# A one-core attention and long-convolution kernel: rotated sines, a check at the end in place of a branch at the start, and a new order of the work

## The chip, the cores and the metric

The kernel runs on one core of one Trainium2 chip. The core has five instruction streams that this text names as the profile does: PE (TensorE: matmuls; its weight loads are the rows PEld), DVE (VectorE), ACT (ScalarE), POOL (GpSimd) and SP (SyncE, which only issues transfers here). Work passes between them through SBUF and through PSUM, whose eight banks the kernel uses as four slots of two banks. The metric is device time in microseconds (us) of one execution; lower is better. Times quoted from the profile are of one execution of the kernel before the change.

## What is computed

Attention over 4 batches, 8 heads, 768 positions and head width 64, and then a gated long convolution on the 512 columns that the heads make together:

```python
scores = scale * q @ k.T                       # per batch and head
mask = causal                                  # heads with is_retrieval
     or causal & (key < 4 | q - key < 64)      # the other heads
a = softmax(where(mask, scores, -1e9))
x = concat_heads(a @ v)                        # (4, 768, 512)
x1, x2, x3 = split(x @ w_proj)                 # three of (4, 768, 512)
conv = irfft(rfft(x2, axis=1) * rfft(filter_fft, axis=0)[None])
out = (x1 * conv * x3) @ w_out                 # (4, 768, 512), float32
```

## The kernel before, in words

After some constants (`opening`, L895) the kernel compares the flags `is_retrieval` with the pattern that it was written for (`check`, L1849) and leaves the result, one number, in `other`. L1862 loads that number into a register on all five engines, and L1863 branches: `general` serves any pattern, `patterned` (from L1036) the expected one. The data at hand has the expected pattern, so `patterned` is what runs and what the profile shows.

`patterned` treats the heads in 16 pairs n, four to a batch. For a pair, SP loads q, k and v (L1401, L1404, L1423; three buffers each), an engine casts q and k to bfloat16 (`cq`, `ck`, helper lines L1101 on DVE, L1103 on POOL, L1107 on ACT), and they are transposed: for the first eight pairs by PE (`T`, L1447), with a copy out of PSUM behind it (`E`), for the later eight by a DMA_TRANSPOSE that SP issues (L1457). `kx` and `vx` pick out the keys and values that the far blocks need. `sc` (L1492) makes blocks of scores, for pairs 0 to 3 with the mask added as a matmul of a table of large negative numbers, `btab` (`sb`, L1505; the table is made on POOL at L1165 to L1183 and scaled on DVE at L1187); `ex` (L1511) is the exponential on ACT, `mk` the other masks on DVE, `at` (L1556) the product with v, which carries a column of ones that yields the row sums, `rec` (L1562) their reciprocals, `nm` (L1573) the scaling.

The convolution over 768 positions is a real Fourier transform done with matmuls: attention's result is folded into symmetric and antisymmetric parts (`fd`, `fe`, `fA`, `fS`, `fb`, `fr`, helper line L1110 and L1601), multiplied by a table of cosines and sines `G` of 3 blocks of 128 positions (`W`, L1617), projected (`X`, L1660), multiplied by the filter's spectrum (`pa`, `pb`, `pc`), brought back with the transposed table `Gi` (`c`, L1725), gated with x1 and x3 (L1695; `g`, `cv`, `y`), and multiplied by `w_out` (`o`, L1758). The filter's own transform is `lfilt` (a load of 768 KB by POOL's queue, L1264), `fold` (L1281, L1285) and `F` (L1293). The table is made at the start: `turns`, `angle`, `wrap`, `size` and four groups of Sin on ACT (L1192 to L1214), each over all three blocks; `Gt` (L1254) transposes it on PE.

The order is written out by hand: `FAST` is a list of words such as `sc0.4@1` or `ck0/v`, operation, then PSUM slot (@0 to @3) or engine (/v DVE, /p POOL, /s ACT, /d transfer). Each engine runs its instructions in the order in which the list puts them, and waits at each for what it reads or overwrites. `BLANKS` (L120) gives the sizes of the filler groups: matmuls of 512 columns whose result nobody reads (L1143). The last 128 rows of the output (`HALVED`) are made in two halves of 256 columns (L1754), which are copied out of PSUM by DVE and ACT and stored by SP (L1776) and by ACT's own queue. L1897 is what ends the program on every engine.

## Time and profile before

| what | us |
|---|---|
| three runs | 188.15, 187.84, 187.33 |
| median | 187.84 |
| the profiled execution, its span | 188.0 |
| busy: PE, DVE, ACT, POOL | 171.7, 152.6, 143.3, 64.1 |
| HBM read, written (MB) | 24.64, 6.29 |

The span runs from the first to the last event of the profiled execution. An engine's busy time leaves out branches, register loads and the issuing of transfers. In the rows of instructions the columns are start, duration, engine, line, operation and tiles, and in square brackets the idle time before and what ended it; in the rows of waits they are the time waited in all, the number of times, and the longest. The chain of waits lists, in order of time, what the end of the program hung on.

### The profile page before, as it was taken

To read this page: it belongs to the slowest core of one execution; us is meant where nothing else is said; L and a number is where in the kernel's file an instruction comes from. 1 tells how busy PE (TensorE), PEld (TensorE's weight loads), DVE (VectorE), ACT (ScalarE), POOL (GpSimd) and SP (SyncE) were. 2 spreads that over 40 slices of the span, in tenths; PEclk is the share of its full clock that TensorE was granted. 3 is DMA by queue.
4 is the path that set the end of the run, shared out by engine and by line. 5 is a ranking of instruction groups with operands and counts; after the bars stand their busy time and mean duration, and the time that the engine had idled before them with its cause. 6 is when DMAs were issued, how large, how long until landed. Compare 5 with 4: busy or idle time off the path is not lost.

```text
span 188.0 us, 4376 instructions
## 1 busy us (share of the span) xinstructions
PE 171.7 (91%) x1688; PEld 103.9 (55%) x1704; DVE 152.6 (81%) x301; ACT 143.3 (76%) x191; POOL 64.1 (34%) x96
## 2 busy tenths in 40 slices
PE   0889996989999999999999999999999999999960
PEld 0346773644585556565556656475567644565430
DVE  6559676968999998998799999999799996388720
ACT  6689995879997998987999999899895526613330
POOL 3368750992080094443210111311406405400200
PEclk9999999999999999999999999999999999999998
DMA  5999999699999899999899988688942205300363
GB/s 182 309 271 281 194 187 287 151 260 228 218 210 203 180 192 210 184 232 234 193 249 257 225 180 176 137 138 225 127 125 55 112 2 157 122 3 0 113 248 104
DMA packets 77695, 33.67 MB, mean 179 GB/s; under 512 B 66850, under 2 KB 74082, under 8 KB 77666
## 3 DMA queue, kind: packets, MB, share of 16 engines
q1 hardware_dynamic: 74576, 30.29, 70.4%
q0 software_dynamic: 2944, 2.88, 10.1%
q8 instruction: 15, 0.25, 0.6%
q10 hardware_dynamic: 146, 0.13, 0.2%
q14 instruction: 14, 0.11, 0.2%
HBM read 24.64 MB, written 6.29 MB: 165 GB/s over the span
## 4 chain that ended last, share of the span: by engine, by line
PE 65%; DVE 14%; DMA 7%; POOL 4%; ACT 3%; issue 2%; SPq 0%; POOLq 0%; DVEq 0%
PE f_x_ps L1695 18%; PE f_X_ps L1660 10%; PE f_out_ps L1758 8%; PE f_c_ps L1725 7%; PE f_sc L1492 6%; PE f_att L1556 6%; DMA qk_ahead<-in_q_dram 4%; DMA f_qk_f<-in_q_dram 3%; DVE f_attn L1573 2%; ACT f_pT L1511 2%; PE f_W_ps L1617 2%; DVE f_P L1110 2%; PE f_sc L1505 2%; DVE f_fo L1110 1%; DVE turns L1736 1%
## 5 line engine op out<-in xcount | busy, mean ns | idle before, releaser
L1511 ACT ACTIVATE f_pT<-f_sc 128x1024 bf16<-128x1024 f32 (+3 forms) x68 | 58.7, 918 | 3.7 <-PE f_sc L1492 3.2
L1695 PE MATMUL f_x_ps<-f_xT,f_wproj 128*128 128x384 bf16 x256 | 46.7, 326 | 0.4 <-DVE f_attn L1573 0.3
L1695 PEld LDWEIGHTS <-f_wproj 128*128 128x128 bf16 x256 | 23.9, 98 | 16.5 <-issue 1.6
L1660 PE MATMUL f_X_ps<-f_wproj,f_xh 128*128 128x512 bf16 x92 | 22.3, 379 | 0.2
L1758 PE MATMUL f_out_ps<-f_wout,f_gy 128*128 128x512 bf16 x86 | 21.7, 379 | 0.3
L1492 PE MATMUL f_sc<-f_qkT 64*128 64x128 bf16 (+3 forms) x248 | 20.3, 250 | 0.0
L1725 PE MATMUL f_c_ps<-f_Gi,f_P 128*128 128x384 bf16 x96 | 18.4, 326 | 0.2 <-DVE f_gy L1714 0.2
L1110 POOL TENSOR_TENSOR f_fo<-f_attn 128x384 bf16<-128x384 bf16 x13 | 12.3, 954 | 15.0 <-DVE f_attn L1573 14.8
L1736 DVE TENSOR_TENSOR turns<-angle,f_c_ps 128x384 bf16<-128x384 f32 x32 | 16.3, 548 | 1.3 <-PE f_c_ps L1725 0.8
L1556 PE MATMUL f_att<-f_v_aug,f_pT 128*128 128x65 bf16 x392 | 17.2, 193 | 0.0
L1556 PEld LDWEIGHTS <-f_pT 128*128 128x128 bf16 x472 | 16.0, 97 | 2.1 <-issue 0.4
L1107 ACT COPY f_o<-f_out_ps 128x1024 f32<-128x1024 f32 (+2 forms) x12 | 10.2, 854 | 8.7 <-PE f_out_ps L1758 7.8
L1573 DVE TENSOR_TENSOR f_attn<-f_att,f_rec 128x768 bf16<-128x768 f32 x16 | 15.3, 955 | 0.6
L1492 PEld LDWEIGHTS <-f_qkT 64*128 64x128 bf16 x248 | 10.6, 94 | 9.3 <-issue 7.0
L1660 PEld LDWEIGHTS <-f_xh 128*128 128x128 bf16 x96 | 9.0, 98 | 10.3 <-issue 0.7
L1107 ACT CAST f_xh<-f_W_ps 128x768 bf16<-128x768 f32 x13 | 10.5, 807 | 4.5 <-PE f_W_ps L1617 2.3
L1758 PEld LDWEIGHTS <-f_gy 128*128 128x128 bf16 x92 | 8.6, 98 | 9.3 <-DVE f_gy L1718 0.3
L1107 ACT CAST f_X<-f_X_ps 128x1024 bf16<-128x1024 f32 x10 | 10.2, 1016 | 4.6 <-PE f_X_ps L1660 4.5
L1531 DVE TENSOR_TENSOR f_pT<-f_pT,mtab 128x1024 bf16<-128x1024 bf16 (+1 forms) x18 | 12.1, 688 | 1.4 <-ACT f_pT L1511 1.4
L1447 PE MATMUL f_qkT_ps<-identity,f_qk_bf 128*128 128x128 bf16 x96 | 7.9, 225 | 5.6 <-DVE f_qk_bf L1101 5.2
L1725 PEld LDWEIGHTS <-f_P 128*128 128x128 bf16 x96 | 9.0, 98 | 6.5 <-issue 0.6
L1110 POOL TENSOR_TENSOR f_br<-f_fo,f_uv 128x256 bf16<-128x256 bf16 x6 | 4.6, 765 | 21.3 <-DVE f_uv L1110 12.3
(132 smaller groups left out, 329.9 us busy)
## 6 DMA issues: line engine op xcount, KB each, us to landing
f_v_f<-in_v_dram SPq DMA_DIRECT2D x32, 192.0 KB, 4.4
out_dram<-f_o SPq DMA_DIRECT2D x17, 256.0 KB, 2.3
qk_ahead<-in_k_dram SPq DMA_DIRECT2D x6, 384.0 KB, 6.3
qk_ahead<-in_q_dram SPq DMA_DIRECT2D x6, 384.0 KB, 6.3
qk_ahead<-in_k_dram SPq DMA_DIRECT2D x10, 192.0 KB, 4.3
qk_ahead<-in_q_dram SPq DMA_DIRECT2D x10, 192.0 KB, 4.9
f_wproj<-in_moe_w_proj_dram POOLq DMA_DIRECT2D x6, 256.0 KB, 7.2
out_dram<-f_o SPq DMA_DIRECT2D x3, 512.0 KB, 4.4
```

The source lines that it names most:

```text
L1107: nc.scalar.copy(out=out, in_=in_)
L1110: (nc.gpsimd if now["engine"] == "p" else nc.vector).tensor_tensor(out, a, b, op)
L1492: nc.tensor.matmul(sc[:, bank, col:col + 128 * cnt], lhsT=keys, rhs=qkT(n)[rows, 0, 128 * i:128 * (i + cnt)], start=(col == 0 or not biase ...
L1511: nc.scalar.activation(out=pT(n)[:, c, :, 0:w], in_=held[f"sc.{n}.{c}"][:, :, 0:w], func=AF.Exp, scale=SCALE)
L1531: nc.vector.tensor_mul(some, some, near(c)[:, None].to_broadcast([128, 2, cols, 128]))
L1556: nc.tensor.matmul(att[:, hh, 65 * i:65 * i + 65], lhsT=pT(n)[:, c, bank, col:col + 128], rhs=values, start=(z == 0), stop=(z == len(here) ...
L1573: nc.vector.tensor_mul(attn(n).rearrange("p i hh d -> p hh i d"), rows[:, :, :, 0:64], held[f"rec.{n}"][:, :, :, None].to_broadcast([128, ...
L1660: nc.tensor.matmul(ps[:, u, :], lhsT=xh(b)[:, cc, chain, 128 * part:128 * part + 128], rhs=wproj()[:, cc, DM:2 * DM], start=(cc == 0), sto ...
L1695: nc.tensor.matmul(ps[:, s, 0:HS], lhsT=wproj()[:, cc, part * DM + cb * 128:part * DM + (cb + 1) * 128], rhs=xT(b)[:, cc, s * HS:s * HS + HS],
L1725: nc.tensor.matmul(ps[:, r, 0:HS], lhsT=P(b)[:, t, u, ch], rhs=Gi()[:, tile_no], start=(m == 0), stop=(m == 2))
L1736: fn(conv[:, half * HS:half * HS + HS], held[f"evs.{b}.{cb}"], held[f"c_ps.{b}.{cb}"][:, 1, 0:HS])
L1758: nc.tensor.matmul(ps[:, i % 2, :], lhsT=gy(b)[:, cb, i * 128:(i + 1) * 128], rhs=wout()[:, cb, :], start=(cb == 0), stop=(cb == NC - 1))
```

## The change

1. **One path in line.** `general` is rewritten as a slow version with loops whose transfers all go by GpSimd's queue. The branch at the start is gone; `patterned` always runs. At its end the kernel decides whether the result may stand: all reciprocals of row sums are kept in one array (`recs`), `gd0` to `gd2` on DVE test that each lies between 2^-100 and 2^100, `gd3` (a matmul of one column) counts the rows where that holds, `gd4` joins it with the flags' comparison, and `flag` loads it into a register on all engines; only if it is not 0 does `general` run behind. The mask table goes from 2^15 to 2^100 for this.
2. **Rotated sines.** Only the first of the three blocks of the table is made with `turns`, `wrap`, `size` and Sin; the other two follow by rotation by a third of a turn (`gc`, `gr`, `gm`, `gs`: a copy, scaled copies and scaled sums, most of them on DVE).
3. **Fillers.** Seven filler matmuls (`warm`) stand at the very start of PE's stream; the 17 that were in three groups are in eight.
4. **The last rows.** The two halves of the last 128 rows have a PSUM tile each.
5. **The order.** `FAST` is drawn up anew: engines, slots and order of many operations differ. The number of matmuls is the same but for the seven fillers and `gd3` (1704 before, 1712 now).

```diff
-BLANKS = (8, 3, 6)
+WARM = 7
+BLANKS = (2, 2, 2, 2, 3, 2, 2, 2)
+FAR = 2.0 ** 100
+LEAST = 2.0 ** -100
...
+    @op("warm")
+    def _():
+        ps = psum.tile([128, 512], FP32, name="warm")
+        for _ in range(WARM):
+            nc.tensor.matmul(ps, lhsT=blank()[:, 0:128], rhs=blank(), start=True, stop=True)
...
-            src = (size if part == 0 else angle)()[:, :, lo:hi].rearrange("p m (r f) -> p m r f", r=2)
+            src = (size() if part == 0 else angle()[:, 0])[:, lo:hi].rearrange("p (r f) -> p r f", r=2)
...
+    @op("gc")
+    def _():
+        ev(G()[:, :, 0], base())
+    for i in range(2):
+        scaled(f"gr{i}", lambda i=i: turned()[:, :, i], lambda i=i: base()[:, 1 - i:5 - i:3], KAPPA if i == 0 else -KAPPA)
+    for u in range(2):
+        for m in range(1, NM):
+            @op(f"gm{u}.{m}")
+            def _(u=u, m=m):
+                tiles = slice(3 * u, 3 * u + 2)
+                nc.vector.scalar_tensor_tensor(
+                    out=G()[:, tiles, m], in0=base()[:, tiles], scalar=0.5 if (u, m) == (0, 1) else -0.5,
+                    in1=turned()[:, u], op0=ALU.mult, op1=ALU.subtract if (u, m) == (1, 2) else ALU.add)
...
+    @op("gd0")
+    def _():
+        nc.vector.tensor_scalar(out=sane(), in0=recs().rearrange("p n h t -> p (n h t)"), scalar1=LEAST, scalar2=None,
+                                op0=ALU.is_ge)
...
+    @op("gd2")
+    def _():
+        nc.vector.tensor_reduce(out=right()[:, 0:1], in_=sane(), op=ALU.min, axis=mybir.AxisListType.X)
+    @op("gd3")
+    def _():
+        nc.tensor.matmul(banks("rows_right")[0:1, 0, 0:1], lhsT=right()[:, 0:1], rhs=v_aug(0)[:, 0, 0, 64:65],
+                         start=True, stop=True)
+    @op("gd4")
+    def _():
+        nc.vector.tensor_scalar(out=pre["other"], in0=held["rows_right"][0:1, 0, 0:1], scalar1=128.0,
+                                scalar2=pre["differ"], op0=ALU.not_equal, op1=ALU.max)
+    @op("flag")
+    def _():
+        pre["reg"] = nc.values_load(pre["other"][0:1, 0:1], min_val=0, max_val=1)
...
+                        ps = banks(f"out_ps.{b}.{i}.{half}")
...
+    patterned(tc, ahead, pre, q, k, v, int(n_sink), int(window), moe_w_proj, moe_filter_fft, moe_w_out, out)
+    with tc.If(pre["reg"] != 0, preferred_fallthrough_block=False):
+        general(tc, local, q, k, v, int(n_sink), int(window), moe_w_proj, moe_filter_fft, moe_w_out, out)
```

How the order changed is shown at four places. A row is line, operation, output tile, input tiles and shape of one instruction, or of several alike (x2).

On ACT, the stretch from the constants to the first exponential (`f_pT` is an exponential's output, `f_qk_bf` a cast q and k, `f_qkT` a transposed one, `f_G` and `f_base` the sines). Before:

```order
L1862 TENSOR_LOAD other
L1863 COMPARE_AND_BRANCH
L1192 ACTIVATE turns<-fcol,tfrac 128x384 x2
L1214 ACTIVATE f_G<-angle 128x3x2x64
L1107 COPY f_qkT_3005<-f_qkT_ps_2983 128x768
L1214 ACTIVATE f_G<-angle 128x3x2x128
L1214 ACTIVATE f_G<-f_size,quarter 128x3x2x64
L1107 CAST f_qk_bf_2972<-qk_ahead_68 128x768
L1214 ACTIVATE f_G<-f_size,quarter 128x3x2x128
L1107 COPY f_qkT_3051<-f_qkT_ps_3029 128x768 x2
L1511 ACT_TABLE_LOAD
L1511 ACTIVATE f_pT_3076<-f_sc_3_3048 128x2x384
```

and now:

```order
L552 CAST f_qk_bf_139<-qk_ahead_66 128x768
L471 ACTIVATE turns<-fcol,tfrac 128x384
L691 ACTIVATE f_base<-angle 128x2x64
L691 ACTIVATE f_base<-angle 128x2x128
L691 ACTIVATE f_base<-f_size,quarter 128x2x128
L552 COPY f_qkT_166<-f_qkT_ps_152 128x768
L684 ACTIVATE f_turned<-f_base 128x2x128
L691 ACTIVATE f_base<-f_size,quarter 128x2x64
L1006 ACT_TABLE_LOAD
L1006 ACTIVATE f_pT_199<-f_sc_4_188 128x1024
```

Four copies and casts stood among the sines, two stand there now, one of them the cast of the first k, and a scaled copy for the rotation; the sines are over one block and no longer three.

On POOL, from the first cast on (`mtab` is the mask table, `f_v_aug` the values with their column of ones, `f_kx` the picked keys; the last operand of a cast is the buffer of the load that it waits for). Before:

```order
L1103 CAST f_qk_bf_2972<-qk_ahead_68 128x768
L1103 CAST f_qk_bf_2974<-qk_ahead_65 128x768
L1383 MEMSET f_v_aug_2979 128x12
L1103 CAST f_qk_bf_3009<-f_qk_f_2_2977 128x768
L1379 MEMSET f_kx_3011 128x4x64
L1383 MEMSET f_v_aug_3036 128x12
L1165 AFFINE_SELECT mtab<-mtab 128x3x128
L1170 MEMSET mtab 4x128
L1171 AFFINE_SELECT mtab<-mtab 128x3x128
L1178 AFFINE_SELECT mtab<-mtab 128x3x128
L1183 MEMSET mtab 4x3x128
```

and now:

```order
L448 AFFINE_SELECT mtab<-mtab 128x3x128
L633 MEMSET mtab 4x3x128
L453 MEMSET mtab 4x128
L548 CAST f_qk_bf_139<-qk_ahead_66 128x768
L454 AFFINE_SELECT mtab<-mtab 128x3x128
L878 MEMSET f_v_aug_174 128x12
L704 TENSOR_SCALAR f_base<-par 128x1
L878 MEMSET f_v_aug_197 128x12
L878 MEMSET f_v_aug_206 128x12
L548 CAST f_qk_bf_208<-qk_ahead_69 128x768
L548 CAST f_qk_bf_249<-f_qk_f_2_135 128x768 x2
```

The mask table stood behind three casts, the last of them of pair 2 (`f_qk_f_2`); now only its last step stands behind one, of pair 0.

On SP, the loads and the first transposes by transfer of pairs 8 and up (`f_xT` and `f_Xw` are other tiles; the three `f_qkT` are of pairs 8, 9 and 10). Before:

```order
L1457 DMA_TRANSPOSE f_qkT_3844<-f_qk_bf_3842 128x12x128
L1404 DMA qk_ahead_65<-in_k_dram 128x6x64 x2
L1404 DMA qk_ahead_65<-in_q_dram 128x6x64 x2
L1423 DMA f_v_f_7_3972<-in_v_dram 128x6x64 x2
L1404 DMA qk_ahead_68<-in_q_dram 128x6x64 x2
L1423 DMA f_v_f_8_4076<-in_v_dram 128x6x64 x2
L1457 DMA_TRANSPOSE f_qkT_4099<-f_qk_bf_4094 128x12x128
L1423 DMA f_v_f_10_4274<-in_v_dram 128x6x64 x2
L1457 DMA_TRANSPOSE f_qkT_4282<-f_qk_bf_4161 128x12x128
```

and now:

```order
L899 DMA qk_ahead_66<-in_k_dram 128x6x64 x2
L918 DMA f_v_f_7_1183<-in_v_dram 128x6x64 x2
L952 DMA_TRANSPOSE f_qkT_1242<-f_qk_bf_1204 128x12x128
L899 DMA qk_ahead_69<-in_k_dram 128x6x64 x2
L952 DMA_TRANSPOSE f_qkT_1345<-f_qk_bf_1299 128x12x128
L918 DMA f_v_f_8_1355<-in_v_dram 128x6x64 x2
L899 DMA f_qk_f_11_1364<-in_k_dram 128x6x64 x2
L952 DMA_TRANSPOSE f_qkT_1458<-f_qk_bf_1382 128x12x128
```

The three transposes by transfer stood with ten loads between the first and the second; now two loads stand there, and they come closer together, behind more of the loads of pairs 8 to 10.

On DVE, the end of the program now (`f_c_ps` and `f_x_ps` are results of L1725 and L1695, `f_out_ps_5_0` and `f_out_ps_5_1` the PSUM tiles of the halves, `f_o` what is stored):

```order
L555 TENSOR_TENSOR turns<-turns,f_x1s_3_2886 128x768
L1213 TENSOR_TENSOR f_gy_2769<-turns,f_x_ps_3_2890 128x768
L661 TENSOR_SCALAR other<-f_rows_right,differ 1x1
L546 COPY f_o_0_2922<-f_out_ps_1_2900 128x512
L546 COPY f_o_2_2934<-f_out_ps_5_0_2916 128x256
L666 TENSOR_LOAD other
L546 COPY f_o_2_2934<-f_out_ps_5_1_2949 128x256
L1363 COMPARE_AND_BRANCH
```

Of these, the row of L661, the register load and the copy of one half by itself ahead of the other are new; the branch stands here and no longer at the start.

1036 lines of the change are left out of this document (288 added, 748 removed).

## The prediction

> **What bounds the kernel now.** I read the page first: the busy shares, the slices, the chain that ended last.
>
> ```profile
> PE 171.7 (91%) x1688; PEld 103.9 (55%) x1704; DVE 152.6 (81%) x301; ACT 143.3 (76%) x191; POOL 64.1 (34%) x96
> ...
> PE 65%; DVE 14%; DMA 7%; POOL 4%; ACT 3%; issue 2%; SPq 0%; POOLq 0%; DVEq 0%
> ```
>
> PE is busy for 91% and makes up 65% of the chain: what can be won is where it idles or runs fillers, or behind its last matmul, since the change keeps every matmul. The stretches show where (length, then busy time of PE, PEld, DVE, ACT, POOL, then PE's clock, the share of the DMA engines, GB/s).
>
> ```profile
> 0.00:8.00 8.00, 2.78 (x12) 1.46 (x13) 5.67 (x22) 4.58 (x8) 1.98 (x12) 1.00 0.70 221
> ...
> 16.00:24.00 8.00, 7.68 (x141) 5.64 (x141) 5.99 (x12) 7.75 (x11) 6.61 (x10) 1.00 1.02 244
> 24.00:32.00 8.00, 6.47 (x98) 4.52 (x100) 5.28 (x12) 6.78 (x9) 1.94 (x5) 1.00 0.98 234
> 32.00:40.00 8.00, 7.22 (x88) 4.37 (x89) 6.28 (x9) 5.14 (x7) 7.09 (x11) 1.00 0.89 191
> ...
> 80.00:112.00 32.00, 31.62 (x354) 19.60 (x353) 29.29 (x62) 29.38 (x38) 6.86 (x11) 1.00 1.05 224
> ```
>
> Between 80 and 112 us PE misses 0.38 of 32, but ACT and DVE are at 29.4 and 29.3 there and the transfers take the whole of the 16 DMA engines (1.05): a stage with PE first and three others close behind. PE's waits of the first 48 us, asked by themselves, and its first rows:
>
> ```profile
> PE f_qkT_ps L1447 <- DVE f_qk_bf L1101: 5.2, 1, 5.2
> PE f_F_ps L1293 <- DVE f_fold L1285: 1.4, 1, 1.4
> PE f_sc L1492 <- POOL f_kx L1103: 0.6, 1, 0.6
> PE f_sc L1505 <- DVE f_btab L1187: 0.5, 1, 0.5
> PE f_qkT_ps L1447 <- POOL f_qk_bf L1103: 0.4, 1, 0.4
> ```
>
> ```profile
> 5.22 0.80 PE L1447 MATMUL f_qkT_ps<-identity,f_qk_bf 128*128 128x128 bf16 x6 [5.22 <-DVE f_qk_bf L1101]
> 5.81 3.60 PE L1143 MATMUL f_blank_ps<-blank 128*128 128x512 bf16 x8
> ...
> 11.73 1.46 PE L1143 MATMUL f_blank_ps<-blank 128*128 128x512 bf16 x6
> ```
>
> After the 5.2 us for the first load these waits are only 2.9 us. But PE is busy with fillers too: 3.60 us for eight (0.45 each), 1.46 for six (0.24 each), while the kernel waits for the first scores.
>
> **The head.** The chain of waits shows why the first scores come late, and ACT's rows what that does.
>
> ```profile
> 3.78 5.97 DMA f_qk_f<-in_q_dram
> 9.80 0.82 POOL f_qk_bf L1103
> ...
> 13.20 0.41 DVE f_btab L1187
> 13.65 0.27 PE f_sc L1505 x2
> ```
>
> ```profile
> 8.89 0.82 ACT L1107 CAST f_qk_bf<-qk_ahead 128x768 bf16<-128x768 f32 x1
> ...
> 10.45 0.78 ACT L1107 COPY f_qkT<-f_qkT_ps 128x768 bf16<-128x768 bf16 x1
> ...
> 12.75 1.28 ACT L1511 ACT_TABLE_LOAD   x1
> 14.04 2.64 ACT L1511 ACTIVATE f_pT<-f_sc 128x768 bf16<-128x768 f32 x3
> ```
>
> ```profile
> L1214 ACT ACTIVATE f_G<-angle x2: 523/684/845, 6.5 to 7.6; 128x384 bf16<-128x384 f32 x1, 128x768 bf16<-128x768 f32 x1
> ```
>
> The mask table is queued on POOL behind the cast of pair 2, whose load lands at 9.75; so the first masked scores are at 13.65 and the first exponential at 14.04. Afterwards ACT is full (7.75 of 8 between 16 and 24 us). In the new order the table stands behind one cast of pair 0 only, and ACT has three sines of 384 columns or fewer where it had four over three blocks. Step by step: PE's first transposes at 5.2 show that k of pair 0 is in and cast by then; ACT's cast of 0.82 may end near 5.0, `turns` on ACT and `wrap` on DVE (384 columns each, at the 0.52 of a sine of that size 0.55 or so) at about 6.1. Three sines (0.31 for 128 columns, 0.42 for 256, on the line through the row's 0.52 and 0.85, so 1.15), a copy of 0.78, a scaled copy and the last sine (0.7 together) end near 8.7. The table load of 1.28 puts the first exponential at about 10.0, 4.0 us earlier. Its scores are ready: second cast on POOL (0.82) by 6, transposes and copy 0.6 + 0.95, scores about 8.1. Bounds: 2 us earlier if the scores wait for the sines' copy on ACT, 4.5 if all is at its shortest.
>
> ACT carries about 0.6 us of other work between these exponentials that it did not carry before (the order has `ks2` there and a cast of pair 3 near the end), so by the end of pairs 0 to 2's exponentials I count 3.4 us. PE does not win all of that: 18 transposes of the table (`Gt`) lay in its shadow and now come later, 1.0 us by the two chain rows that follow, and 0.3 is left for slots. **PE gains 2.1 us here** (1.0 to 3.2).
>
> ```profile
> 15.12 0.67 PE f_Gi_ps L1254 x12
> ...
> 22.92 0.34 PE f_Gi_ps L1254 x6
> ...
> 26.53 7.03 DMA qk_ahead<-in_q_dram
> 33.61 0.83 POOL f_qk_bf L1103
> ...
> 41.75 0.65 PE f_blank_ps L1143 x3
> ```
>
> **The next stage, 24 to 48 us.** PE waits 1.4 us for the filter's fold and 0.6 for a `kx`, which by the chain hangs on a load issued at 26.5 and a late cast at 33.6. The filter's load and those of pair 5 stand earlier in the new list; but DMA's share is 0.98 and 0.89 there, so earlier issue is shared out. I take both waits as gone (2.0), with nothing as the low end. The third group of fillers (0.65) goes too; six of the new fillers stand later, between real work, at 0.22 each: 1.3 us lost. Into PE's stream comes one matmul of one column, nothing. New waits in a plan that has not been seen: between nothing and 3 us; I take 0.75, the nearest rows being the waits above of 0.4 to 1.4, each alone.
>
> **The rotation, the guard and POOL.** The sums of the rotation, four of them, two scaled copies and four plain ones, are about 4 us on DVE at the price of its copies of 768 columns (0.55 to 0.96); DVE is idle for 1.7 to 2.7 of each 8 us quoted before 40, so they cost nothing unless the transform's first matmuls come before them. The guard on DVE is two passes of 192 columns and a reduction, under 1 us by the price of its smaller rows (a fold of 384 columns is 0.395, below), on an engine that is busy for 81% of the span and idles 0.99 us before its last copy (in the tail's rows). Cover gone, each is at most its own length. POOL takes 7 or so more of the gating and folding operations.
>
> ```profile
> L1110 POOL TENSOR_TENSOR f_fo<-f_attn 128x384 bf16<-128x384 bf16 x13 | 12.3, 954 | 15.0 <-DVE f_attn L1573 14.8
> L1110 DVE TENSOR_TENSOR f_fo<-f_attn 128x384 bf16<-128x384 bf16 x19 | 7.3, 395 | 0.2
> ```
>
> A fold is 0.56 us longer there, on an engine that is 34% busy: a longer chain to each transform, inside the 0.75 above.
>
> **PE's end** by the sum: 2.1 + 2.0 + 0.65 - 1.3 - 0.75 = 2.7 us earlier, 1.2 to 4.2 by the bounds taken together.
>
> **The tail.**
>
> ```profile
> 181.64 0.42 DVE L1101 COPY f_o<-f_out_ps 128x256 f32<-128x256 f32 x1 [0.99 <-PE f_out_ps L1754]
> 182.10 0.37 ACT L1107 COPY f_o<-f_out_ps 128x256 f32<-128x256 f32 x1 [0.70 <-DVE f_o L1101]
> 182.50 0.40 ACTq L1776 DMA_DIRECT2D out_dram<-f_o  x1
> ```
>
> ```profile
> L1863 ACTq COMPARE_BRANCH  x2: 38/42/45, 3.7 to 182.9; - x2
> ```
>
> ```profile
> L1897 ACTq DRAIN  x2: 8/44/80, 187.0 to 187.4; - x2
> out_dram<-f_o ACTq DMA_DIRECT2D x1, 128.0 KB, 3.0
> ```
>
> The last two copies share a PSUM tile and run one after the other; the tiles of their own let the first go out early, and only one copy of 0.42 and one store of 3 us stay behind the last matmul: 0.4 us gained (0.46 for the second copy, less the register loads, which took 0.47 to 0.54 at the start and now stand between copies). ACT leaves its last branch at 182.9 and does nothing until 187.0, 4.1 us, longer than the store needs (182.5 + 3.0 = 185.5): the end hangs on that idle stretch, behind a jump over the other block's code (some 180 rows on ACT). Now the jump is over about 40 rows. If the stretch stays at 4.1, ACT's earlier end is worth 0.4 to 0.8; if it goes, the store's landing decides, up to 1.8. I take **1.0**. [...] The branch at the start cost its row loads (about 0.5) off PE's path, since PE waits for the load of k there until 5.2.
>
> **Sum.** Profiled span 188.0 - 2.7 - 1.0 = 184.3; that execution lies 0.16 above the median of 187.84, so 184.1.
>
> **Rivals.**
>
> *A. Given back.* The head's 4 us only let PE run into the stage of 48 to 112 us earlier, where ACT, DVE and the transfers are at 0.91 to 1.05. For it: the three rows of load in that stretch; against: the new list takes copies and casts of some 5 us from ACT, PE was the one that others waited for. If the whole 2.7 is lost, the tail remains: 188.0 - 1.0 - 0.16 = 186.8; if half, 185.5; with new waits also eating the tail, 187.8.
>
> *B. Slower.* The transposes by transfer of pairs 8, 9 and 10.
>
> ```profile
> L1457 SPq DMA_TRANSPOSE f_qkT<-f_qk_bf x8: 1391/1665/3304, 56.0 to 123.0; - x8
> DMA to landing us min/median/max: 3.7/4.2/7.1
> ```
>
> ```profile
> 69.77 1.14 PE L1617 MATMUL f_W_ps<-f_G,f_fo 128*128 128x384 bf16 x6
> ```
>
> Now the first is issued at 56.0 and its scores come after these transform matmuls, at about 72: 16 us. In the new order some 4 us of PE's work lie between the two places (the projections, products and transforms in between at this trace's prices), and the first three stand almost back to back behind loads. At the median of 4.2 that just fits; at 7.1 each is 3.1 late, on PE's path, three times 9.3: 193. It decides from 1.6 us a transpose, where the gain is gone and 0.5% more (188.8). With two of three late: 184.1 + 6.2 = 190.3. [...]
>
> *C. Both ends at their best.* Waits of the early stage gone, no new ones, and the idle stretch at the end gone: 188.0 - 4.2 - 1.8 - 0.16 = 181.8.
>
> *D. The sines' part does nothing.* If the first scores wait for PE's transposes or copies, not for ACT, the head gains 2 rather than 4: PE 1.0 rather than 2.1, so 185.2; within the forecast's spread.
>
> **How the numbers follow.** Forecast with D's smaller head (183 to 186): 0.55. C (below 183): 0.13. A beyond half (186 to 188.8): 0.21, some 0.09 of it below 186.9. B: 0.11. About 0.5% is what a measurement of this kernel can tell from no change, 186.9 to 188.8. Faster: 0.55 + 0.13 + 0.09 = 0.77; within: 0.12; slower: 0.11. The range reaches from C's best, 181.8, into A, 187.6, and leaves out B and the rest of A.
>
> **What would show it.** The first exponential at 10 us, not 14, and the last of pair 2 three us earlier; no wait of over 0.5 us for the fold or `kx` before 45; the transforms' first matmuls not behind the rotated table; PE's busy share over 97% between 40 us and its end, with no wait on f_qkT of a later pair; the last matmul near 179; ACT's stretch behind L1363 shorter than 4.1. I am wrong if PE's end is later than 181, or if DVE or ACT is over 95% in 48 to 112 while PE falls below.

## The result, and the profile after

| | before | after |
|---|---|---|
| runs, us | 188.15, 187.84, 187.33, 187.65 | 193.65, 193.01, 193.45, 193.05 |
| median | 187.75 | 193.25 |
| ratio, 95% interval | | 1.0279 [1.0227, 1.0331] |
| span of the profiled execution | 188.0 | 191.5 |
| last matmul ends | 181.6 | 185.6 |

The change made the kernel slower by 5.5 us; 184.1 was forecast, and the range ended at 187.6. Run again beside the kernel before it gave 1.031 (below, `e9_after_again`). The two profiles lie only 3.5 us apart. In the runs of the kernel before that stand beside the experiments the time is 1.7 to 1.8 us above the span, and by that the profiled execution of before, with a span of 188.0, was some 2 us longer than a median one; the forecast took its span for a time near the median. Differences in place and length are read from the profiles here, the size of the loss from the medians. (The profile of `e3_fill` below is of an execution that the comparisons leave out as disturbed; only places are read from it.)

The page after, busy time, the clock by slices and the chain's shares:

```profile
PE 176.4 (92%) x1712; PEld 105.1 (55%) x1712; DVE 165.9 (87%) x318; ACT 140.6 (73%) x182; POOL 74.1 (39%) x98
...
PEclk9969999999999999999999999999999999999996
...
PE 75%; DVE 11%; DMA 5%; ACT 4%; issue 2%; DVEq 0%
```

PE is busier by 4.7 us with the same useful matmuls (the fillers take some 2.5 us more, a stretch of 3.41 us at half clock up to 1.7, and 16 matmul records of the profile before are missing, x1688 of 1704), DVE by 13.3 and POOL by 10. The clock has a dent in the third slice (0.50 is granted from 10.44 to 13.85 us). PE's waits over the whole program (time waited, times, longest):

```profile
PE f_blank_ps L593 <- DVE f_Gi L546: 1.9, 1, 1.9
PE warm L463 <- DVE blank L382: 1.5, 1, 1.5
PE f_sc L987 <- DVE f_xh L546: 1.4, 1, 1.4
PE f_qkT_ps L942 <- ACT f_qkT L552: 1.1, 1, 1.1
PE f_sc L987 <- DVE f_xT L546: 0.7, 1, 0.7
PE f_sc L987 <- DVE f_qkT L546: 0.7, 1, 0.7
PE f_qkT_ps L942 <- DVE f_qk_bf L546: 0.6, 1, 0.6
```

The waits for the fold and for `kx` are gone, as forecast. In their place PE waits for DVE four times behind the head (4.6 us), and none of its longer waits is for a transfer. The stretches (length, busy time of PE, PEld, DVE, ACT, POOL, PE's clock, DMA share, GB/s):

```profile
8.00:16.00 8.00, 6.72 (x57) 3.85 (x57) 4.77 (x12) 6.71 (x9) 3.81 (x5) 0.79 1.00 268
16.00:24.00 8.00, 7.43 (x138) 5.49 (x136) 7.39 (x10) 7.40 (x11) 6.20 (x9) 1.00 1.06 247
24.00:32.00 8.00, 6.51 (x98) 4.89 (x97) 6.82 (x12) 5.65 (x8) 4.78 (x8) 1.00 1.10 256
32.00:40.00 8.00, 6.67 (x85) 4.09 (x83) 7.35 (x14) 6.01 (x9) 2.29 (x4) 1.00 0.97 195
40.00:48.00 8.00, 6.82 (x52) 3.00 (x50) 7.53 (x8) 7.95 (x10) 5.21 (x7) 1.00 0.93 195
80.00:112.00 32.00, 32.00 (x367) 19.28 (x366) 29.95 (x68) 28.93 (x38) 7.79 (x11) 1.00 1.20 211
```

Between 80 and 112 us PE has no gap, and from 48 to 176 us it is idle for 1.2 us in all (1.1 before): most of the loss is made before 48 us, where DVE has 0.5 to 1.2 us of each 8 left from 16 on (1.7 to 2.7 were read before). The largest single piece stands on DVE's timeline (start, duration, engine, line, operation, tiles):

```profile
21.05 0.41 DVE L719 SCALAR_TENSOR_TENSOR f_G<-f_base,f_turned 128x256 bf16<-128x256 f32 x1
21.39 3.28 DVE L743 COPY f_Gh<-f_G 128x384 bf16<-128x384 bf16 x1
24.70 0.18 DVE L747 TENSOR_SCALAR f_Gh<-f_G 128x6 bf16<-128x6 bf16 x1
24.78 0.55 DVE L546 COPY f_Gi<-f_Gi_ps 128x768 bf16<-128x768 bf16 x1
```

The same copy before:

```profile
18.61 0.47 DVE L1240 COPY f_Gh<-f_G 128x384 bf16<-128x384 bf16 x1
```

And POOL after, in those microseconds:

```profile
20.16 0.82 POOL L548 CAST f_qk_bf<-qk_ahead 128x768 bf16<-128x768 f32 x1
20.93 1.04 POOL L767 DMA_DIRECT2D f_filt<-in_moe_filter_fft_dram  x1
21.97 0.84 POOL L548 CAST f_v_aug<-f_v_f 128x768 bf16<-128x768 f32 x1
22.76 1.78 POOL L555 TENSOR_TENSOR f_fo<-f_attn 128x384 bf16<-128x384 bf16 x2
```

The copy takes 3.28 us instead of 0.47 and ends at 24.67, right behind POOL's last fold (24.54). The copy of `f_Gi` stands behind it on DVE, and PE, whose next fillers overwrite the transposes' bank, waits 1.9 us for that.

### The profile page after: what moved, and what is told of

Same layout as the page of the kernel before. It is cut to its first block, busy times and chain, and to the rows that moved or that the text cites. A ratio compares the mean times of both kernels' runs of the same rounds, so it can differ in the third digit from the quotient of the medians.

```text
span 191.5 us, 4423 instructions
## 1 busy us (share of the span) xinstructions
PE 176.4 (92%) x1712; PEld 105.1 (55%) x1712; DVE 165.9 (87%) x318; ACT 140.6 (73%) x182; POOL 74.1 (39%) x98
## 4 chain that ended last, share of the span: by engine, by line
PE 75%; DVE 11%; DMA 5%; ACT 4%; issue 2%; DVEq 0%
PE f_x_ps L1190 21%; PE f_out_ps L1255 11%; PE f_X_ps L1155 9%; PE f_sc L987 7%; PE f_att L1051 7%; PE f_c_ps L1220 6%; DMA f_qkT<-f_qk_bf 3%; PE f_qkT_ps L942 3%; PE f_xt_ps L1124 2%; PE f_sc L1000 2%; DMA qk_ahead<-in_k_dram 2%; DVE f_Gh L743 2%; DVE f_HAB L682 2%; DVE f_qk_bf L546 1%; PE f_W_ps L1104 1%
## 5 line engine op out<-in xcount | busy, mean ns | idle before, releaser
L1006 ACT ACTIVATE f_pT<-f_sc 128x1024 bf16<-128x1024 f32 (+2 forms) x68 | 59.1, 913 | 8.2 <-PE f_sc L987 4.3
L1255 PE MATMUL f_out_ps<-f_wout,f_gy 128*128 128x512 bf16 x92 | 24.0, 380 | 0.0
L555 POOL TENSOR_TENSOR f_fo<-f_attn 128x384 bf16<-128x384 bf16 x11 | 10.8, 988 | 21.7 <-PE f_qkT_ps L942 7.7
L555 POOL TENSOR_TENSOR f_uv<-f_fo 128x256 bf16<-128x256 bf16 x11 | 7.8, 719 | 26.5 <-DVE f_fo L555 11.3
L555 POOL TENSOR_TENSOR f_gy<-turns,f_gy 128x768 bf16<-128x768 bf16 x6 | 10.0, 1671 | 19.5 <-issue 9.7
L1231 DVE TENSOR_TENSOR turns<-angle,f_c_ps 128x384 bf16<-128x384 f32 x32 | 16.5, 547 | 1.1 <-PE f_c_ps L1220 0.6
L552 ACT COPY f_o<-f_out_ps 128x1024 f32<-128x1024 f32 (+1 forms) x13 | 11.5, 887 | 6.6 <-PE f_out_ps L1255 5.3
L1068 DVE TENSOR_TENSOR f_attn<-f_att,f_recs 128x768 bf16<-128x768 f32 x16 | 15.3, 953 | 0.5
L1026 DVE TENSOR_TENSOR f_pT<-f_pT,mtab 128x1024 bf16<-128x1024 bf16 (+1 forms) x18 | 14.6, 830 | 0.4 <-ACT f_pT L1006 0.4
L552 ACT CAST f_X<-f_X_ps 128x1024 bf16<-128x1024 f32 x11 | 11.1, 1012 | 5.1 <-PE f_X_ps L1155 5.1
L552 ACT CAST f_xh<-f_W_ps 128x768 bf16<-128x768 f32 x15 | 12.1, 805 | 3.6 <-PE f_W_ps L1108 3.0
```

The costliest lines, as they stand in the source:

```text
L552: nc.scalar.copy(out=out, in_=in_)
L555: (nc.gpsimd if now["engine"] == "p" else nc.vector).tensor_tensor(out, a, b, op)
L1006: nc.scalar.activation(out=pT(n)[:, c, :, 0:w], in_=held[f"sc.{n}.{c}"][:, :, 0:w], func=AF.Exp, scale=SCALE)
L1026: nc.vector.tensor_mul(some, some, near(c)[:, None].to_broadcast([128, 2, cols, 128]))
L1068: nc.vector.tensor_mul(attn(n).rearrange("p i hh d -> p hh i d"), rows[:, :, :, 0:64], recs()[:, n][:, :, :, None].to_broadcast([128, 2, N ...
L1231: fn(conv[:, half * HS:half * HS + HS], held[f"evs.{b}.{cb}"], held[f"c_ps.{b}.{cb}"][:, 1, 0:HS])
```

## The experiments

### The same kernel again

```diff
(none)
```

> The change as it is, as the control for the others on their chip, since the kernel before itself ran 188.6 to 189.1 us beside the experiments against 187.75 at first. Every theory: ratio to the kernel before 1.023 to 1.033. What it tells: whether the gains of the slow block left out (ratio 1.0127), the folds on DVE (1.0124) and the fillers in the early wait (1.0176) are gains or chips.

Measured 1.031 [1.0232, 1.0388]. Its profile has the same wait of 1.9 us for `f_Gi`, but the clock's fall lies at 33 us and not at 10. The result stands; where the clock falls varies.

### What holds the table copy

`e2_gh_reduce` puts another form of instruction in the copy's place (a maximum over one element), at the same place of the order.

```diff
-        nc.vector.tensor_copy(out=Gh(), in_=G()[:, 5])
+        nc.vector.tensor_reduce(out=Gh().rearrange("p m f -> p (m f)"), in_=G()[:, 5].rearrange("p m (f o) -> p (m f) o", o=1),
+                                op=ALU.max, axis=mybir.AxisListType.X)
```

> One instruction has another form: the copy of 128x384 from the table that took 3.28 us on DVE at 21.4 (0.47 for the same copy before the change) is a maximum over one element, same operands, same place. In the change it ran while POOL had a transfer issue, a cast and two folds in a row without a break, until 24.54. Theory A, the copy in DVE's fast form waits for POOL to leave a gap: the new form takes about 0.5 us at 21.4, PE's wait of 1.9 us at 23 is gone, and the time falls by 1.5 to 2.0, to 191.3 to 191.8. Theory B, the copy waited for its operand or for a write before it to be visible: the new form takes as long, time 193.0 to 193.5. Theory C, DVE is full there in any case: the wait goes, another takes its place, time 192.7 to 193.3.

1.0189 [1.0122, 1.0256]. DVE's timeline:

```profile
21.28 0.53 DVE L743 TENSOR_REDUCE f_Gh<-f_G 128x384 bf16<-128x384 bf16 x1
21.85 2.63 DVE L748 TENSOR_SCALAR f_Gh<-f_G 128x6 bf16<-128x6 bf16 x1
```

and POOL's last row beside it:

```profile
22.66 1.78 POOL L555 TENSOR_TENSOR f_fo<-f_attn 128x384 bf16<-128x384 bf16 x2
```

The reduction is not held, but the scaling of 6 columns behind it, 0.18 before, takes 2.63 and ends with POOL's folds again (24.48 and 24.44). So neither the tile nor the size tells what is held: beside the same row of POOL's the copy took 3.28 and the scaling 2.63, the reduction 0.53. Nor is the copy held beside any work of POOL: before, it took 0.47 at 18.61 and was over while a transfer issue of POOL's ran from 18.91 to 19.95. The hold only moved: PE still waits 1.7 us for `f_Gi`, and the interval overlaps that of the change, so this run's time decides nothing.

`e6_folds_on_dve` takes the two folds from POOL and gives them to DVE, which is fuller.

```diff
-... lq4 fe0/p rec1 ... Gt0@1 fd0/p tn0@3 at2.0@0
+... lq4 fe0/v rec1 ... Gt0@1 fd0/v tn0@3 at2.0@0
```

> The change with two folds (fe0, fd0; 0.9 each on POOL, 0.4 on DVE) given to DVE, so that POOL's row without a break behind the filter's transfer issue ends near 22.8 and not at 24.5. Theory A, the copy of the table on DVE waits until POOL leaves a gap (with another form of that copy, which took 0.53, the next small scaling behind it took 2.63 in its place): the copy ends by 23.0, 1.6 us earlier, PE's wait there falls from 1.9 to under 1.0; time 0.5 to 1.5 us below the change, 4.0 to 5.0 above the kernel before. Theory B, DVE has too much to do there: the 0.8 us more on DVE cancels it, time within 0.3 us of the change.

1.0124 [1.0055, 1.0193], some 3 us off the change. DVE's copy and POOL's rows:

```profile
20.08 1.54 DVE L743 COPY f_Gh<-f_G 128x384 bf16<-128x384 bf16 x1
```

```profile
18.85 0.82 POOL L548 CAST f_qk_bf<-qk_ahead 128x768 bf16<-128x768 f32 x1
19.62 1.04 POOL L767 DMA_DIRECT2D f_filt<-in_moe_filter_fft_dram  x1
20.66 0.84 POOL L548 CAST f_v_aug<-f_v_f 128x768 bf16<-128x768 f32 x1
```

POOL's streak now ends at 21.50, and the copy ends at 21.62. Three kernels, three lengths (3.28, 2.63, 1.54), and each time the held instruction ends 0.04 to 0.13 us behind POOL's last one. PE's wait for `f_Gi` falls from 1.9 to 0.2:

```profile
PE f_blank_ps L593 <- DVE f_Gi L546: 0.2, 1, 0.2
```

The clock stays whole in this profile until the end of the work (0.988 in the mean over the whole execution, with the end in it), and the last matmul ends at 181.8. Of the 3.8 us by which that is earlier than in the change, 1.8 are less idle time of PE; of the other 2, the matmuls and fillers that no longer run at half clock make at most 1.7 (half of 3.41); how much of the 3 us in the medians is the hold alone is not shown. The same meeting is seen later in the changed kernel, on DVE's timeline:

```profile
45.73 2.04 DVE L1026 TENSOR_TENSOR f_pT<-f_pT,mtab 128x768 bf16<-128x768 bf16 x1
47.69 0.94 DVE L546 CAST f_xh<-f_W_ps 128x768 bf16<-128x768 f32 x1
```

```profile
46.73 0.61 POOL L775 DMA_DIRECT2D f_wproj<-in_moe_w_proj_dram  x1
47.34 1.11 POOL L548 CAST f_v_aug<-f_v_f 128x768 bf16<-128x768 f32 x1
```

This mask product, 0.54 at its shortest, takes 2.04 beside five casts and issues that stand back to back on POOL from 44.57 to 48.45, and the cast behind it is what PE waits 1.4 us for. Here the hold did not last until POOL paused: the product ends at 47.77, and POOL's cast beside it takes 1.11 us instead of 0.83 or 0.84. Why DVE is held is not shown: the rows tell only what ran at the same time and which ended first. The 3.28 us are longer than any single instruction of POOL beside them (1.04 at most): the hold lasted over a whole row of them.

Over the whole profile of the change 17 DVE instructions lie more than 0.3 us above the shortest of the same form in these profiles, by 16.8 us together; before it was 6, by 3.2 us. The difference is about as large as DVE's 13.3 us more. Half of it lies behind 125 us, where PE goes on almost without a gap, so that only the early ones can be seen in PE's waits.

### The clock and the fillers

`e3_fill` makes the groups at the head larger, `e4_no_late_fillers` takes away three groups, `e10_no_warm` the seven at the start.

```diff
-BLANKS = (2, 2, 2, 2, 3, 2, 2, 2)
+BLANKS = (2, 2, 2, 2, 8, 5, 2, 2)     e3_fill
+BLANKS = (0, 2, 0, 2, 3, 2, 0, 2)     e4_no_late_fillers
-... fcol1 ident warm mtab0v quarter ...
+... fcol1 ident mtab0v quarter ...    e10_no_warm
```

> Eight more filler matmuls in the two places where PE waits between 7.0 and 10.2 us (five and three); nothing else. In the change PE's clock is full from 7.0, half from 10.4 to 13.9, full again. Theory A, the clock falls because PE was idle for most of the stretch before: no fall, the first scores at full pace, PE's useful work at 16 us about 1 us ahead of the change; the time falls by 0 to 1.0 (192.3 to 193.3), less than it gains since the copy on DVE at 21 holds PE afterwards. Theory B, the fall comes from the load of the fillers themselves: it stays or comes earlier, and the time is the same or up to 1 us longer.

> The three filler groups of two matmuls that stand in the middle of the stream are empty (31 us once, 77 us twice). Theory A, after 48 us PE has no idle time to put them in, so four of them are plain loss: 0.86 us less from 77 us on and 0.2 to 0.4 from the first, time 192.0 to 192.5. Theory B, the plan is bound by DVE (29 to 31 of 32 us busy from 80 on) and PE only waits elsewhere: time 193.0 to 193.4.

> The change without the seven fillers at the start. Theory A, they bring PE's clock up before there is work, the clock's watch then sees an idle stretch (7.0 to 10.2 us) and halves it for 3.4 us in the middle of the first scores: without them the clock comes up later, near 9 to 13 us, and doesn't fall at once; PE's useful work at 16 us is level with the change within 0.7 us, and the time is within 1 us of the change (the copy held by POOL at 21 sets the pace in both). Theory B, the fillers are a gain that the fall only cuts: 0.5 to 1.7 us longer than the change.

Measured: 1.0176 [1.0101, 1.0251], 1.0273 [1.0213, 1.0333] and 1.0275 [1.0221, 1.0329]. With larger groups at the head the clock keeps whole there (1.00 between 8 and 16 us instead of 0.79) and falls between 32 and 40 instead (0.79):

```profile
32.00:40.00 8.00, 7.20 (x76) 3.98 (x75) 5.88 (x11) 4.74 (x6) 1.19 (x3) 0.79 1.01 204
```

Taking fillers away wins nothing: in `e4_no_late_fillers` PE stands idle where they stood, and without the seven there are two falls. The fillers are not what the change loses by. Nor is a fall the main loss. By an estimate from the change's profile, a stretch of 3.41 us at half clock takes 0.9% off an execution's mean clock (1.7 of 191.5 us), so executions with a mean of 0.995 or more had none before the end. Four such are on record in `e2_gh_reduce` and `e3_fill`, with times of 191.66 to 193.2 us; the three at 0.983 to 0.990 beside them, on the same chip, took 190.91 to 192.49, so in these few a higher clock did not go with a shorter time.

### The slow block behind the end

`e1_no_slow_path` drops the branch and the block.

```diff
-    with tc.If(pre["reg"] != 0, preferred_fallthrough_block=False):
-        general(tc, local, q, k, v, int(n_sink), int(window), moe_w_proj, moe_filter_fft, moe_w_out, out)
```

> The change without the slow block behind the guard (the guard and the register loads stay; nothing follows them, so other flags would not be served). The change's time, 193.25, is 1.5 to 2.2 us above its profiled span, and an 8 KB instruction packet goes out 2.2 us after the span's last event, where the kernel before has its last one inside the span. Theory A, the slow block's code lies between the last instruction and what ends the program, and fetching it is paid behind the span: time about 191.3, within 0.3 of its span, PE's last matmul unchanged at 185.6. Theory B, the gap belongs to the guard's register loads or to how long the program is: time 193.0 to 193.4, gap still about 2.

1.0127 [1.0067, 1.0187]: 2.9 to 3.4 us less than the change. Neither theory fits as written: the time still lies 1.7 us above the span, and what goes is inside the span. 1.7 of it is the tail, 4.27 us from the last matmul to the end of the span instead of 5.96. The DMA queues from 176 us on (packets, MB, share), of the changed kernel and of this one:

```profile
q1 hardware_dynamic: 1152, 1.97, 31.6%
q10 hardware_dynamic: 144, 0.13, 2.3%
q14 instruction: 5, 0.04, 0.9%
q8 instruction: 1, 0.02, 0.4%
```

```profile
q1 hardware_dynamic: 1152, 1.97, 30.8%
q10 hardware_dynamic: 144, 0.13, 2.2%
```

With the jump, packets of instructions go out among the last stores (the rows q14 and q8: six packets, 0.06 MB, 1.3% of the DMA engines' time there), without it none; ACT's own store of 128 KB takes 3.8 us to land instead of 2.3. The rest of the gain lies in PE's end, 183.6 instead of 185.6, with the fall at 24.9 us instead of 10.4; what of that is due to the missing block stays open.

Four runs tried the other side, the kernel before. `e5_before_no_branch` calls `patterned` directly, and `e11_no_branch_in_order` puts four fills first on POOL besides.

```diff
-    with tc.If(reg != 0, preferred_fallthrough_block=False) as cmp:
-        general(tc, ahead, pre, q, k, v, is_retrieval, n_sink, window, moe_w_proj, moe_filter_fft, moe_w_out, out)
-    with cmp.Else():
-        patterned(tc, ahead, pre, q, k, v, int(n_sink), int(window), moe_w_proj, moe_filter_fft, moe_w_out, out)
+    patterned(tc, ahead, pre, q, k, v, int(n_sink), int(window), moe_w_proj, moe_filter_fft, moe_w_out, out)
...
-angle1 turns1 angle2 ck1/p cq0/p turns2 lq2 ones0 ck0/v ...
+ones0 kz2 ones2 ones1 angle1 turns1 angle2 ck1/p cq0/p turns2 lq2 ck0/v ...    e11_no_branch_in_order
```

> The kernel before with its fast block alone: the register load stays, the branch and the general block are left out (other flags would not be served). Theory A, the jump over the other block at the end costs: code packets of 8 and 16 KB are fetched for it by the same DMA engines that carry the last stores, so the stretch from PE's last matmul to the end of the span falls from 6.4 us to about 4.3, as it did when the slow block was left out of the change (5.96 to 4.27); time 1.6 to 2.2 us below the kernel before. Theory B, the stretch is set by the stores' own landing (3.1 us) and what ends a program: 0 to 0.5 us below. Either way this is the measure for the new plan without its branch: if the new plan is as good, its version without the slow block (ratio 1.0127 to the kernel before) stands level with this one; I expect it 3 to 4 us above.

> As e5_before_no_branch (the kernel before, its fast block alone; other flags would not be served), but with four short fills on POOL put ahead of the first cast there, since in e5 that cast, waiting for its load, stood ahead of the identity matrix, and PE's first transposes came at 8.5 us where the kernel before has 5.2. Theory A, the branch and the jump cost what the stretch after the last matmul showed (6.4 us before, 3.6 in e5): first transposes at 5.2 or earlier, ratio 0.980 to 0.988. Theory B, the gain at the end was bought at the start: ratio over 0.995. Against the repaired new plan without its slow block (ratio 0.9967) this says which plan is the better one.

`e5_before_no_branch` gave 1.0032 [0.9993, 1.0071], no gain, although its tail is 3.63 us: without the branch as a border POOL took the first cast, which waits for a load, ahead of the identity, and PE's first transposes waited for that:

```profile
PE f_qkT_ps L1447 <- POOL identity L1000: 8.5, 1, 8.5
```

With the fills in between, `e11_no_branch_in_order` gave 0.989 [0.985, 0.9929], the fastest run of the study, with the last matmul at 180.9 and the same tail. It serves the expected flags only.

`e8_before_slow_first` and `e12_before_short_slow` keep a branch in the kernel before, but with the short slow block; the one jumps to `patterned` at the start, the other has it in line and jumps over the block at the end.

```diff
-def general(ctx, tc, first, pre, q, k, v, is_retrieval, n_sink, window, ...
+def general(ctx: ExitStack, tc, local, q, k, v, n_sink, window, ...
...
-    with tc.If(reg != 0, preferred_fallthrough_block=False) as cmp:
+    with tc.If(reg != 0, preferred_fallthrough_block=True) as cmp:     e8_before_slow_first
...
-st3.3 o3.5.0@3 o3.5.1 oe3.5/v st3.5 oe3.6/s st3.6/s
+st3.3 o3.5.0@3 o3.5.1@1 oe3.5/v st3.5 oe3.6/s st3.6/s             e12_before_short_slow
```

> The kernel before, its plan untouched, with the change's short slow block in place of the general one, placed ahead of the fast block: the jump is taken at the start, over some 40 rows on ACT, and nothing is jumped over at the end. Theory A, the jump at the end costs 1.6 to 2.2 us because its code fetch shares the DMA engines with the last stores, and the jump at the start is over in time for the first load (PE waits for it until 5.2 anyway): time 1.2 to 2.2 us below the kernel before. Theory B, a jump costs the same wherever it stands: the start is 1.5 to 2 us later, time within 0.5 us of the kernel before.

> The kernel before and its plan with two parts of the change alone: the short slow block in place of the general one, where that stood (behind the fast block, the branch at the start), and the two halves of the last rows with a PSUM tile each. Theory A, ACT's idle stretch of 4.1 us behind its last branch becomes short as in the change (0.4), the first half's store goes early, and the stretch after the last matmul falls from 6.4 to between 5.0 and 6.0: 0.4 to 1.4 us below the kernel before, ratio 0.992 to 0.998. Theory B, the code fetch still shares the DMA engines with the last stores: within 0.3 us of the kernel before.

1.0154 [1.0083, 1.0226] and 0.9976 [0.9932, 1.002]. At the start the jump costs most, against both theories: its code comes at 7.2 to 9.3 us, among the first loads, DVE stands idle for 5.48 us across its branch, and PE's first transposes start at 11.2 us instead of 5.2:

```profile
9.23 1.47 DVE L688 TENSOR_SCALAR angle<-fcol,tcol 128x384 f32<-128x384 f32 x2 [5.48 <-issue]
```

A shorter block at the end, as the change has it, saves nothing that can be told: the tail is 6.0 us, with a PSUM tile for each half. What counts at the end is whether there is a jump at all (6.0 and 6.4 us of tail with one, 3.6 without).

### The change repaired

`e7_repaired` joins what was found: no slow block, the two folds on DVE, larger groups at the head in place of three later ones, and one copy ahead of the mask product.

```diff
-BLANKS = (2, 2, 2, 2, 3, 2, 2, 2)
+BLANKS = (0, 2, 0, 2, 8, 5, 0, 2)
...
-... lq4 fe0/p rec1 ... Gt0@1 fd0/p tn0@3 at2.0@0
+... lq4 fe0/v rec1 ... Gt0@1 fd0/v tn0@3 at2.0@0
...
-sc5.1@3 sc4.0@1 ex4.2 cv5/p mk5.2 lw2.1 We3/v ck6/p ...
+sc5.1@3 sc4.0@1 ex4.2 cv5/p We3/v mk5.2 lw2.1 ck6/p ...
...
-    with tc.If(pre["reg"] != 0, preferred_fallthrough_block=False):
-        general(tc, local, q, k, v, int(n_sink), int(window), moe_w_proj, moe_filter_fft, moe_w_out, out)
```

> The change with all that was found so far put right: slow block left out (other flags would not be served), two folds on DVE, fillers in the early wait and none later, one copy out of PSUM moved ahead of the mask product that waited for POOL at 45.7. Theory A, the new order's loss is in these places: PE's waits between 20 and 50 us sum to under 2.5 us (6 in the change), PE's clock doesn't fall or falls once, last matmul at 181.5 to 182.5, time 0 to 1.5 us below the kernel before, and level with or up to 1 us above the kernel before without its branch. Theory B, each cure lets the next engine's wait out (DVE carries 13 us more than before): last matmul after 183, time over 1 us above the kernel before.

0.9967 [0.9929, 1.0004]: the 5.5 us are back, as the two parts alone would have it (1.55% and 1.5%). But it is no faster than the kernel before, and 0.8% behind `e11_no_branch_in_order`, the old kernel freed of the same jump (the two intervals just meet). Only the folds, the fillers and the copy mend the change; the jump at the end stands in the kernel before as well, so leaving it out gives back nothing that the change had lost. With the jump in both kernels 1.24% are left (`e6_folds_on_dve`). Its waits:

```profile
PE f_sc L987 <- DVE f_xT L546: 1.4, 1, 1.4
...
PE f_qkT_ps L942 <- ACT f_qkT L552: 1.1, 1, 1.1
PE f_sc L987 <- ACT f_xT L552: 0.7, 1, 0.7
PE f_sc L987 <- DVE f_xh L546: 0.6, 1, 0.6
PE f_X_ps L1155 <- ACT f_o L552: 0.5, 1, 0.5
```

The meeting of the two engines is not over in it: at 41.35 us a cast on DVE, 0.54 at its shortest in this run, takes 2.18 beside POOL's casts and issues.

### The parts or the order

Four runs put the change's parts into the order of before: `e13_old_order`, and `e14_old_order_no_slow` without the block; `e15_old_order_mended` and `e16_mended_no_slow` are the same with two faults of the first list mended.

```diff
-angle1 turns1 angle2 ck1/p cq0/p turns2 lq2 ones0 ck0/v wrap1 T0.1@0 wrap2 blank0@1 wrap0 ...
+ck1/p cq0/p lq2 ones0 ck0/v T0.1@0 blank0@1 wrap0 ...                             e13_old_order
+ones0 kz2/p ones2 ones1 mtab3 ck1/p cq0/p lq2 ck0/v T0.1@0 blank0@1 wrap0 ...     e15_old_order_mended
...
-lq3 ex0.4 Gt0@1 Ge0/v ck3/v sc0.1@2 ...
+lq3 ex0.4 ck3/v gc/v sc0.1@2 ...
...
+... Gt1@0 lk8 Ge1/v Gt0@1 Ge0/v lk4 ...                                           e13_old_order
+... F1.0@3 Gt0@0 Ge0/v blank1@0 sc4.4@1 ...   (BLANKS = (8, 0, 6))                e15_old_order_mended
```

> The changed kernel's parts (rotated sines, seven fillers at the start, the check at the end with the slow block behind it, a PSUM tile per half) in the order of the kernel before: its list of operations, engines and its three filler groups (8, 3, 6), with the steps of the rotation put between DVE's copies from 14 to 22 us and both groups of table transposes after the second pair's scores. Theory A (the new order is at fault, since it lets POOL and DVE meet; the parts cost little): ratio to the kernel before 0.99 to 1.005, PE's waits after 24 us at most 3 us in all, no copy of the table over 1 us. Theory B (the parts are at fault: some 4 us more of DVE work by the rotation, and the check): ratio 1.015 or more, with PE waiting for DVE over 1 us at least twice between 14 and 48 us.

> The same without the slow block and its branch; flags other than the expected ones are not served. Its counterparts are the new order without the slow block, repaired (0.9967), and the kernel before without its branch (0.989). Theory A (order): 0.975 to 0.99, ahead of the repaired new order by 1 us or more, the tail behind the last matmul 3.6 to 4.3 us. Theory B (parts): 0.995 or more, no better than the repaired new order. If it lies 1.0 to 1.5% below the run with the slow block, the price of the block is the same in both orders.

> The parts in the old order again, with the two faults of e13_old_order's list mended, which its waits show (5.2 us for the identity, because a cast that waits for a load got ahead of it on POOL, and 3.0 us for the second group of table transposes): four fills that need no load and the mask table stand first on POOL, and the second group of transposes takes the place of the three fillers near 42 us. Theory A (order): both waits gone, 4 to 6 us won against e13's 1.041 (more than 5.2 us only if the clock stays whole): 1.01 or less; the rest is the slow block's code. Theory B (the parts themselves): still 1.02 or more with neither of the two waits in the profile, and PE waiting for DVE instead.

> The same without the slow block and its branch; flags other than the expected ones are not served. Theory A: 0.975 to 0.99, as good as the kernel before without its branch (0.989) or better, since the first exponential comes some 2 us earlier. Theory B: 0.995 or more. The tail behind the last matmul 3.6 to 4.3 us in both.

Measured 1.0408 [1.0323, 1.0493], 1.0276 [1.0188, 1.0365], 1.0241 [1.0145, 1.0338] and 1.0053 [0.9993, 1.0113]. The first two tell little, since PE waited 5.2 us for the identity and 3.0 for the second group of transposes. The mended pair speaks against the theory that the new order is to blame: without the slow block the parts give 1.0053 in the old order, 0.9967 in the new one as repaired. They also show what the head hangs on. ACT in `e15_old_order_mended`:

```profile
10.08 0.40 ACT L683 ACTIVATE f_turned<-f_base 128x256 f32<-128x256 f32 x1
10.45 0.80 ACT L551 COPY f_qkT<-f_qkT_ps 128x768 bf16<-128x768 bf16 x1
12.17 0.80 ACT L551 COPY f_qkT<-f_qkT_ps 128x768 bf16<-128x768 bf16 x1 [0.93 <-PE f_qkT_ps L941]
12.99 1.28 ACT L1005 ACT_TABLE_LOAD   x1
14.28 2.64 ACT L1005 ACTIVATE f_pT<-f_sc 128x768 bf16<-128x768 f32 x3
```

The sines are done by 10.1 and POOL's part of the mask table at 4.8, but the first exponential starts at 14.28, as in the kernel before (14.04): the table's scaling on DVE and the load of the exponential's table on ACT stand behind the copies of three pairs. The early head of the change comes from its order, which brings pair 0 alone first. Whether the rotation's DVE work keeps even the repaired kernel behind `e11_no_branch_in_order` is not shown. In `e16_mended_no_slow` PE's longest waits between 9 and 27 us are for POOL's casts and for ACT (2.2, 1.3 and 2.3 us); for DVE there are two of 0.7 later. The lists of these runs placed the rotation's steps by hand, and the price of the slow block, 1.3 and 1.9% in these two pairs, is itself uncertain by about 1%.

## Why the prediction was wrong

**The size of the miss.** The measured 193.25 lies 9.15 us above the forecast. PE's last matmul makes 6.7 of it (185.6 in the profile, 178.9 by the sum) and the tail 0.55. The other 1.9 come from the base: a span was set equal to a median time, and here the median lies 1.75 above the span.

**The head: right mechanism, three quarters of the size, spent at once.** The forecast had the first exponential at 10.0, 4.0 earlier, and 2.1 us for PE. ACT's rows after:

```profile
9.11 1.28 ACT L1006 ACT_TABLE_LOAD   x1
10.91 1.68 ACT L1006 ACTIVATE f_pT<-f_sc 128x1024 bf16<-128x1024 f32 x2 [0.51 <-PE f_sc L1000]
```

It came at 10.9, 3.1 us earlier than before, with the scores made at half clock ahead of it (0.50 from 10.44 us on). PE's first product with v starts at 17.8 instead of 19.1, and at 16.3 to 16.5 in the runs whose clock was whole there (`e6_folds_on_dve`, `e7_repaired`, `e9_after_again`): 2.6 to 2.8 earlier. The wait for `f_Gi` at 23 us took most of it back.

**The early waits: gone, but replaced.** The 2.0 us for the fold and `kx` were won as forecast. The 0.75 for new waits is the term that broke: 4.6 us for DVE alone. Its high bound of 3 was too low as well, and the spread did not use it: the forecast's own low bounds (1.0 for the head, nothing for the early waits, 3 lost to new ones, with 0.65 and 1.3 as they are) put PE's end 2.65 us later, not 1.2 earlier.

**The rotation and POOL: the step that failed.** "DVE is idle for 1.7 to 2.7 of each 8 us quoted before 40, so they cost nothing", and POOL's longer folds "inside the 0.75 above". The two were priced apart, each by the busy share of its own engine. Together they meet: 13.3 us more on DVE and 10 on POOL, and the lengthened instructions on DVE (3.28 for 0.47; 2.04 for 0.54; the count above) are about as much by themselves. The condition that the forecast gave, the transform's first matmuls not behind the rotated table, held; what stood behind the table was the copy of `f_Gi`, and PE behind that. Two folds moved to DVE, by the forecast's prices 0.8 us more on the fuller engine, brought 3 us, part of it perhaps by the clock. That is not all of it: `e7_repaired` ends its last matmul at 182.5, where the sum had 178.9. Its waits behind the head, in the rows above, make 3.2 us (1.4, 0.7, 0.6, 0.5), 2.4 more than the 0.75; the other 1.2 stays open. Of the 2.79% by which the change is slower, 1.24% remain in `e6_folds_on_dve` without a cause that is shown.

**The clock: not a term of the sum.** With seven fillers at the start it is whole from 7.02 us on, before from 9.25 (the matmuls of 512 columns follow each other every 0.43 us ahead of that and every 0.22 behind it). In its two profiles the change is idle for 1.8 and 1.4 us of 3.41 and has a stretch of the same length at half speed behind each; behind 2.0 us of idle time in the 3.41 from 23.4 us on it has none. A fall is at most 1.7 us of work (half of 3.41), and by the runs above not the main loss.

**The tail: wrong.** 1.0 us was forecast, 0.45 is seen in the profile (6.41 to 5.96), and the repeats and the runs that keep the block lie between 5.7 and 6.6. ACT's idle stretch behind its branch did go, from 4.1 to 0.4 us, and then the store's landing decided, as the forecast had it; but it took 3.8 us and not the 3.0 of the sum. What makes the difference is not shown: five packets of instructions go out beside the store in either profile. The number lies in the lower of the forecast's two cases (0.4 to 0.8), but not for the reason given there: ACT did not stand behind its branch.

**The rivals.** *B* named a loss, but in the wrong place: PE waits for none of the transposes by transfer. *A*'s stage from 48 to 176 us did not give anything back (PE idle for 1.2 us of 128, 1.1 before). The rival that was missing is one in which the two cheap-looking engines slow each other, in the stage where both are given more.

## What to carry to other kernels

Work moved to DVE or POOL is not priced by its own duration and the engine's idle share alone: look at what the other of the two does in the same microseconds, and keep POOL's long rows of casts, folds and issues away from DVE copies that PE waits for (here 3.28 us for 0.47). A jump over a block that never runs costs some 2 to 3 us at the end of this kernel (2.1 by `e11_no_branch_in_order`, 2.9 to 3.4 by `e1_no_slow_path`) and more at its start (some 5, `e8_before_slow_first` against `e11_no_branch_in_order`); at the end the short block costs as much as the long one (`e12_before_short_slow`, 0.9976). Where a branch goes, look at what moves up past its place in each queue: a cast that waits for a load held the identity back by 3 us and more here.

## What the hardware showed that was not expected

- A DVE copy and a scaling were held until POOL paused: 3.28, 2.63 and 1.54 us for 0.47, 0.18 and 0.47, ending 0.04 to 0.13 us behind POOL's last instruction. The reduction of the same tile at the same place was not held (0.53). A two-input product (2.04 for 0.54) and a cast (2.18 for 0.54) were held too, but ended within POOL's row, and the POOL casts beside them took 1.11 and 1.22 us instead of 0.83.
- PE's clock fell to half for 3.41 us after stretches with 1.4 to 3.2 us of idle time in the 3.41 us before (eleven falls ahead of the program's end); other stretches of that length with up to 2.0 us idle (the change, from 23.4 us on) had no fall. Idle time in the stretch alone did not tell where a fall comes.
- With a jump at the end the tail is 5.7 to 6.6 us, without one 3.6 to 4.3, in both kernels. From 176 us on packets of instructions of 8 and 16 KB go out among the stores in the change (six) and in the kernel before (eight), none in `e1_no_slow_path`. That they delay the stores would fit the landing times of ACT's last store in the change and in `e1_no_slow_path` (3.8 and 2.3 us), but was not tried by itself; in the kernel before, that store took 3.0 us with as many packets beside it as in the change (five).
